# Half mixers in two streams: turning and angles in every second portion, products in the others

## The chip, the cores and the metric

The kernel runs on one core of one Trainium2 chip. The metric is the time of one execution on the device in microseconds (us); each kernel is run several times and the median is compared. Below, PE is TensorE, PEld its weight loads, DVE VectorE, ACT ScalarE, POOL GpSimd, SP SyncE, which issues DMAs. L368 is line 368 of the kernel before.

## What is computed

Eight batches of attention over 576 positions with 8 heads of width 64. In each row of scores only the 32 largest count. The result goes through a mixer with 512 channels, whose weights are one set for all batches. All of it is float32.

```python
scores = scale * q @ k.T                       # 576 x 576 for each head
attn = softmax(where(scores >= 32nd largest of the row, scores, -1e9))
x = attn @ v                                   # heads side by side: 576 x 512
theta = x @ w_theta
y = w_tok_r @ (x * cos(theta)) + w_tok_i @ (x * sin(theta))
u = x + y
out = u + relu(u @ w_ch)
```

## The kernel before

**Units.** Attention is cut into units of 128 queries of a pair of heads (two score rows of 576 in each partition); the last unit of a pair holds the 64 queries left over, of both heads. A batch has 20 units, the kernel 160. `GROUPS` gives the order within a batch: all five units of pair 0, then the first two of pairs 1 and 2, all five of pair 3, then the last three of pairs 1 and 2. So the queries of the first half (blocks 0 and 1, h = 0) are complete after unit 10 of a batch, those of the second (blocks 2, 3 and the rest, h = 1) after unit 19.

**Steps.** `pipeline` runs one iteration per unit, and each iteration emits steps of several units in the order `ORDER`: P (`penalize`: ACT makes a penalty, POOL subtracts it), T and Z (`threshold`: DVE finds the 32nd largest), U (`turn`: PE transposes the exponentials of the unit before the last, ACT copies them out of PSUM), F (`pick`), K (`keep`: ACT copies a finished product with the values to `xt`), S (`scores` and `fold` of the unit three ahead), V (`mix_values`: product with the values into `px`), M (weights, at the start only), X (`exponent`: ACT, with the sums). Loads of the pairs, their split into high and low parts and the copies into place follow on SP's queue. Eleven buffers of tag `e` hold scores, exponentials and the raw pairs.

**Half mixers.** When the fourth pair of a half is kept (step K), a generator `mixer(bt, h)` is appended to the list `running`. It has two phases:
- turning and angles: for each block the sums get a tiny addend on POOL and DVE takes the reciprocal (L477, L478), PE turns `xt` (`px_s`, L621), DVE scales it into `z` (L515), PE turns it back (`px_t`, L530), ACT copies to `xt` (L532), PE multiplies by `w_theta` (`pth`, `angles`, L558 and L562), ACT and DVE take the fraction of a turn (`fraction`, L574 with the tile `whole`, and L575). Then `trig` does two sines and an absolute value per block on ACT (L583 to L585) and two multiplications on POOL (L586, L591). For h = 1, POOL first adds `part`, the share of the first half (L635).
- products: token products in `py` (L687), 32 of them for h = 0 and 40 for h = 1, of 256 or 320 columns; DVE or ACT takes each finished group of 4 or 5 (`settle`, L662 and L660). For h = 1 follow 32 channel products in `po` (L718); DVE adds and clamps (`give`, L669) into the output tile `ot`, and SP sends it out (L671).

**The order of the work.** Step U calls `advance` twice. Each call draws steps from the first generator of `running` until `RATE / 2` = 4.25 is used up; a product counts its columns over 288, a step of the turning counts `TURN` = 4.25. There is one stream: a half mixer is emitted whole before the next one begins, its sines are followed at once by its products. Two kinds of instructions keep the order in which they were emitted: the transposes of step U and the matmuls of the half mixers on PE (`fixed`), and exponentials and sines on ACT (`tabled`). The rest is ordered by a planner that works through the program with its own estimate of the times, and that prefers the mixer's steps somewhat (`M_REST`).

**Buffers that the change and the argument touch.** `ps_m`, two PSUM buffers, serves `px`, `pth`, `py` and `po`. `whole` and `ot` are one tile in one buffer (tag `ot`). `z0` and `z1` hold one half each, in one buffer. `zt` holds first the sines, then `part`.

The last half mixer (last batch, h = 1) is written another way (`split`): in fast float32 passes over high and low parts, and it runs after all the units.

Of the kernel before, what the change touches and what calls it, by code (L numbers as in the profile page):

```python
# [9 lines left out]
F32 = mybir.dt.float32  # L10
# [8 lines left out]
P = 128  # L19
EBUFS = 11  # L20
NQP = 1
WSTART = 2
AHEAD = 3
S_LATE = 0
RATE = 8.5
TURN = 4.25
ORDER = "PTUFKSTVMXZ"
FOLDS = 4
# [6 lines left out]
M_REST = -100  # L35
# [11 lines left out]
def topk_attention_phase_mixer(  # L47
# [11 lines left out]
    nc = tc.nc  # L59
    B, NPAIR, _, S = qT.shape  # L60
    DM = w_ch.shape[0]
# [3 lines left out]
    NJ = S // P  # L65
    REM = S - NJ * P
# [13 lines left out]
    wk2 = ctx.enter_context(tc.tile_pool(name="wk2", bufs=2))  # L80
# [97 lines left out]
    def later(n):  # L178
        return tc.high_priority(offset=-n)
# [283 lines left out]
    def mixer(bt, h, split=False, beside=False):  # L463
        bq, xt, sums, sums_rem = bt["bq"], bt["xt"], bt["sums"][h], bt["sums_rem"]
        js, j0 = HALVES[h], HALVES[h][0]
        x0 = j0 * P
        full = [j for j in js if j < NJ]
        nf = len(full)
        rinv = wk2.tile([P, len(js), H], F32, tag=f"rinv{h}", name=f"rinv{h}")
# [5 lines left out]
        for rows, ks in regions:  # L475
            tiny = least[:rows].to_broadcast([rows, ks.stop - ks.start, H])
            nc.gpsimd.tensor_add(sums[:rows, ks], sums[:rows, ks], tiny)  # L477
            nc.vector.reciprocal(rinv[:rows, ks], sums[:rows, ks])  # L478

        z = one.tile([P, 2 * nf + len(js) - nf, DM], F32, tag=f"z{h}", name=f"z{h}")  # L480
        zt = []
        if split:
            end = wk2.tile([P, NJ, P], F32, tag="vt", name="end").rearrange("p a b -> p (a b)")
# [81 lines left out]
                            )  # L565

        def fraction(j):
            whole = wk2.tile([P, S], F32, tag="ot", name="whole", bufs=1)[:, :DM]
            if j == NJ:
                last[0] = whole  # L570
            _, zr, _ = spots(j)
            n = zr.shape[-1]
            m = zr.shape[0]
            nc.scalar.activation(whole[:m, :n], th[j][:m, :n], AF.Identity, bias=magic[:m])  # L574
            nc.vector.scalar_tensor_tensor(  # L575
                zr, whole[:m, :n], MAGIC, th[j][:m, :n], op0=ALU.subtract, op1=ALU.subtract
            )
# [36 lines left out]
        for k in range(len(js) + 3):  # L614
            if k < len(js):
                rows = P if js[k] < NJ else REM
                px = ps_t.tile([P, DM], F32, tag="t", name="px_s")
                with later(M_PE):
                    for p in range(NB):
                        fill(  # L620
                            nc.tensor.transpose(  # L621
                                px[:rows, p * P : p * P + P], xt[h][:, p, k * P : k * P + rows], ident
                            )
                        )
                normalize(js[k], px)
            if 0 <= k - 3 < len(js):
                fraction(js[k - 3])
            if 0 <= k - 2 < len(js):
                angles(js[k - 2])
                yield TURN  # L630
            if 0 <= k - 1 < len(js):
                turn_back(js[k - 1])
            yield TURN if k <= len(js) else 0
        if h:
            nc.gpsimd.tensor_add(xt[1], xt[1], bt["part"])  # L635
        trig()
        yield 0
        if not h:
            bt["part"] = spare().rearrange("p (m n) -> p m n", n=QN[1])

# [27 lines left out]
        def give(m, c, ot, y):  # L668
            nc.vector.scalar_tensor_tensor(ot[:, spans[c]], y, 0.0, xt[c][:, m], op0=ALU.max, op1=ALU.add)  # L669
            if c == 1:  # L670
                nc.sync.dma_start(outT[bq, m * P : m * P + P], ot)  # L671

        for m in range(NB):
            for c in range(2):
# [18 lines left out]
                    flush(1)  # L693
        flush()
        if not h:
            return
        for m in range(NB):
            if not split:
                ot = wk2.tile([P, S], F32, tag="ot", name="ot", bufs=1)
            else:  # L700
                if m % 2 == 0:
                    ots = wk2.tile([P, 2, S], F32, tag="kh", name="ots")
                ot = ots[:, m % 2]
            for c in range(2):
                cs, n = spans[c], QN[c]
                po = accumulator(m, c, "po")
                ms = slice(m * P, m * P + P)
                if split:
                    mm = []
                    for kb in range(NB):  # L710
                        mm += passes(
                            *(w[kb][:, ms] for w in w_parts["ch"]), x_hi[c][:, kb], x_lo[kb // 2][:, kb % 2, cs]
                        )
                else:
                    mm = [(wts["ch"][kb][:, ms], xt[c][:, kb]) for kb in range(NB)]
                for i, (l, r) in enumerate(mm):
                    with later(M_TOK if split else 0):
                        fill(nc.tensor.matmul(po[:, :n], l, r, start=(i == 0), stop=(i == len(mm) - 1)))  # L718
                    if not split:
                        yield n / HS  # L720
                        flush()
                late.append(lambda m=m, c=c, o=ot, y=po[:, :n]: give(m, c, o, y))
                if split:
                    flush()
        flush()

    def new_batch(bq):
        sums = [wk2.tile([P, len(js), H], F32, tag=f"sums{h}", name=f"sums{h}") for h, js in enumerate(HALVES)]
        sums_rem = wk2.tile([P, NPAIR], F32, tag="sums_rem", name="sums_rem")
        return dict(bq=bq, sums=sums, sums_rem=sums_rem, xt=[None, None], done=[0, 0])  # L730

    flag = const.tile([1, 1], I32, name="flag")

    def pipeline():
# [6 lines left out]
                plan += [(len(groups) - 1, j) for j in range(ja, jb)]  # L741
        total, per_batch = len(plan), len(plan) // B
        starts = [g[3] for g in groups] + [total]
        units, pairs, batches, running, budget = {}, {}, {}, [], [0.0]
        todo = {}

        def unit(i):
            if not 0 <= i < total:
                return None
            if i not in units:  # L750
                g, j = plan[i]
                b, p = groups[g][:2]
                if b not in batches:
                    batches[b] = new_batch(b)
                    if b % MARKED:
                        batches[b]["marks"] = batches[b - 1]["marks"]
                slot = (b % MARKED * NPAIR + p) * (2 * NJ + 1) + 2 * j
                units[i] = Unit(b, batches[b], p, j, pairs[g], slot, False)
            return units[i]
# [16 lines left out]
            ):  # L776
                todo.setdefault(max(at, 0), []).append((work, g))

        def advance(share):
            budget[0] = min(budget[0] + share, share) if running else 0.0  # L780
            while running and budget[0] > 0:
                with later(M_REST):
                    done = next(running[0], None)
                if done is None:
                    running.pop(0)
                else:
                    budget[0] -= done

# [4 lines left out]
            fold(unit(i))  # L793
        pick(unit(0))
        for i in range(total + 3):
            now, nxt, old, last = unit(i), unit(i + 1), unit(i - 1), unit(i - 2)
            parts = threshold(now) if now else iter(())

            def keep():
                u = unit(i - 3)  # L800
                if u:
                    h = keep_values(u)
                    if h is not None:
                        end = u.bq == B - 1 and h == 1
                        running.append(mixer(u.batch, h, end, not end))

            def ahead():
                if unit(i + AHEAD):
                    with later(S_LATE):
                        scores(unit(i + AHEAD))  # L810
                        fold(unit(i + AHEAD))

            steps = {
                "P": lambda: old and penalize(old),
                "F": lambda: nxt and pick(nxt),
                "T": lambda: next(parts, None),
                "Z": lambda: list(parts),
                "U": lambda: last and turn(last, unit(i - 3), lambda: advance(RATE / 2)),
                "K": keep,
                "S": ahead,  # L820
                "V": lambda: last and mix_values(last),
                "M": lambda: [next(wsteps, None) for _ in range(2 - i % 2)],
                "X": lambda: old and exponent(old),
            }
            for c in ORDER:
                steps[c]()
            done = unit(i - 2)
            if done and (i - 1) % per_batch == 0 and done.bq % MARKED == MARKED - 1:
                judge(done.batch["marks"], done.bq // MARKED)
            for work, g in todo.get(i, ()):  # L830
                work(g)
# [4 lines left out]
        nc.tensor.transpose(pf[:1, :P], worst[:, :1], ident)  # L836
        nc.vector.reduce_max(flag_f, pf[:1, :P], axis=AX.X)
        nc.vector.tensor_copy(flag, flag_f)
        for m in running:
            for _ in m:  # L840
                pass

# [68 lines left out]
```

## Time and profile before

| | us |
|---|---|
| median of 3 runs | 1411.42 (1411.14 to 1418.38) |
| the profiled execution | 1409.92 |
| its span, first to last instruction | 1408.1 |
| PE, DVE, ACT, POOL busy in the span | 1190.7, 1140.4, 1055.4, 726.8 |
| mean granted clock of TensorE | 0.929 of full speed |

A window is a stretch of the span in us from its start. A row of the trace gives first what was busy, then in brackets or behind a bar how long the engine was idle just before and what ended that idle time. PE's busy time counts a matmul from its issue to its modelled end, and matmuls overlap, so the sum of their durations is more than the busy time.

### The profile page before, as it was taken

The numbers are of one execution on the slowest core, as the hardware profiler recorded it, in microseconds if no ns is written. First come the engines' busy times: TensorE is split into PE (matmuls) and PEld (weight loads), VectorE is DVE, ScalarE is ACT, GpSimd is POOL, SyncE is SP. The second block draws the span as 40 slices with busy tenths as digits, with TensorE's granted clock in tenths as the row PEclk, the third lists the DMA queues.
The fourth block names the chain that finished last, engine by engine and source line by source line (L and its number), as shares of the span: only waits on it lengthen the run. The fifth ranks groups of instructions, "written<-read, shape, count | busy, mean of one in ns | idle before, by whom it ended". The sixth has DMA issues, their size and how long they took to land.

```text
span 1408.1 us, 23356 instructions
## 1 busy us (share of the span) xinstructions
PE 1190.7 (85%) x6253; PEld 866.3 (62%) x6253; DVE 1140.4 (81%) x5050; ACT 1055.4 (75%) x2152; POOL 726.8 (52%) x986
## 2 busy tenths in 40 slices
PE   4667788997979989798789979899898988799778
PEld 3445465775657666576566756577565756476458
DVE  7999889789897878879797788979888798977133
ACT  5999696966879486875969668885879769696551
POOL 4688564744556254652737436472546526463340
PEclk9777899999989999999898999899998999999899
DMA  6657233344434342253333434333423534321000
GB/s 176 172 143 205 73 99 85 78 115 104 113 73 100 90 114 73 73 144 92 91 83 78 114 97 111 86 94 87 122 73 73 145 91 114 82 68 43 9 1 36
DMA packets 101996, 134.47 MB, mean 95 GB/s; under 512 B 20320, under 2 KB 59488, under 8 KB 101856
## 3 DMA queue, kind: packets, MB, share of 16 engines
q1 hardware_dynamic: 101856, 132.90, 36.6%
q8 instruction: 52, 0.85, 0.3%
q14 instruction: 88, 0.72, 0.2%
HBM read 47.84 MB, written 9.44 MB: 41 GB/s over the span
## 4 chain that ended last, share of the span: by engine, by line
ACT 28%; PE 25%; DVE 22%; DMA 8%; POOL 6%; issue 6%; SPq 5%; ACTq 0%; POOLq 0%; DVEq 0%
ACT e L368 7%; PE py L687 6%; PE pth L558 5%; PE px L413 5%; ACT pen L355 5%; DVE lst L309 4%; DVE lst L331 4%; POOL e L357 4%; DVE best L325 4%; SPq L230 4%; ACT e L274 3%; PE ps_score L265 3%; PE pt L383 3%; PE po L718 2%; DVE lo L302 2%
## 5 line engine op out<-in xcount | busy, mean ns | idle before, releaser
L357 POOL TENSOR_TENSOR e<-e,pen 128x576 f32<-128x576 f32 x288 | 364.7, 1282 | 132.2 <-ACT pen L355 130.9
L687 PE MATMUL py<-w,z 128*128 128x256 f32 (+1 forms) x1072 | 316.4, 431 | 49.0 <-POOL z L591 46.0
L325 DVE MAX8 best<-lst 128x8 f32<-128x122 f32 (+3 forms) x1152 | 284.0, 287 | 23.5 <-POOL lim L336 22.5
L687 PEld LDWEIGHTS py<-w,z 128*128 128x128 f32 x1072 | 200.7, 201 | 96.1 <-POOL z L591 51.3
L265 PE MATMUL ps_score<-kh,q 128*128 128x288 f32 x512 | 187.4, 379 | 77.4 <-DVE lo L304 45.9
L368 ACT ACTIVATE e<-e,lim 128x576 f32<-128x576 f32 x288 | 223.0, 775 | 26.2 <-POOL e L357 24.8
L331 DVE MATCH_REPLACE8 lst<-best,lst 128x122 f32<-128x122 f32 (+2 forms) x864 | 230.9, 273 | 0.2
L355 ACT ACTIVATE pen<-e,lim 128x576 bf16<-128x576 f32 x288 | 209.5, 770 | 26.7 <-POOL lim L336 23.0
L309 DVE MAX8 lst<-lo 128x8 f32<-128x72 f32 (+1 forms) x864 | 208.5, 292 | 0.1
L383 PE MATMUL pt<-ident,e 128*128 128x128 f32 x1152 | 186.9, 287 | 18.3 <-ACT at L385 8.0
L274 ACT COPY e<-ps_score 128x576 f32<-128x576 f32 x256 | 158.6, 640 | 54.5 <-PE ps_score L265 37.5
L383 PEld LDWEIGHTS pt<-ident,e 128*128 128x128 f32 x1152 | 145.7, 147 | 73.2 <-issue 19.9
L385 ACT COPY at<-pt 128x512 f32<-128x512 f32 x256 | 148.6, 584 | 37.7 <-PE pt L383 35.0
L413 PE MATMUL px<-at,vt 128*64 128x320 f32 (+1 forms) x1024 | 167.5, 450 | 6.6 <-ACT at L388 4.2
L265 PEld LDWEIGHTS ps_score<-kh,q 128*128 128x128 f32 x512 | 104.3, 204 | 101.7 <-issue 42.7
L265 PE MATMUL ps_score<-kl,q 128*128 128x288 f32 x512 | 155.5, 317 | 10.8 <-DMA kl<-raw 10.8
L301 DVE TENSOR_TENSOR ps_score<-ps_score,e 128x288 f32<-128x288 f32 (+1 forms) x160 | 68.3, 427 | 78.7 <-ACT e L274 68.1
L218 POOL TENSOR_TENSOR raw<-raw,hi 128x832 fp32r<-128x832 f32 (+2 forms) x47 | 104.6, 2226 | 52.5 <-ACT hi L217 51.6
L413 PEld LDWEIGHTS px<-at,vt 128*64 128x64 f32 x1024 | 80.0, 149 | 74.6 <-issue 26.8
L718 PE MATMUL po<-xt,w 128*128 128x256 f32 (+1 forms) x448 | 120.7, 407 | 1.6 <-DVE xt L662 1.4
L558 PE MATMUL pth<-w,xt 128*128 128x512 f32 x240 | 111.9, 610 | 8.2 <-ACT xt L532 8.2
L312 POOL COPY marks<-lst 128x6 f32<-128x6 f32 (+1 forms) x160 | 31.1, 195 | 168.5 <-DVE lst L309 164.1
(136 smaller groups left out, 2017.2 us busy)
## 6 DMA issues: line engine op xcount, KB each, us to landing
kh<-hi SPq DMA_DIRECT2D x188, 144.0 KB, 2.5
kl<-raw SPq DMA_DIRECT2D x188, 144.0 KB, 2.6
raw<-in_kT_dram SPq DMA_DIRECT2D x47, 288.0 KB, 3.1
vt<-in_v_dram SPq DMA_DIRECT2D x48, 256.0 KB, 3.0
out_dram<-ot SPq DMA_DIRECT2D x28, 288.0 KB, 2.1
raw<-in_qT_dram SPq DMA_DIRECT2D x15, 288.0 KB, 3.0
q<-hi SPq DMA_DIRECT2D x30, 144.0 KB, 2.8
q<-raw SPq DMA_DIRECT2D x30, 144.0 KB, 2.8
```

The source lines that it names most:

```text
L265: nc.tensor.matmul(out[:, at : at + n], l, r, start=(i == 0), stop=(i == len(mm) - 1), skip_group_check=True)
L274: nc.scalar.copy(u.x[:, :, keys], u.ps[:, :, :HS])
L309: nc.vector.max(u.lst[:, w, QS + i * 8 : QS + i * 8 + 8], u.lo1[:, w, lo:hi])
L325: nc.vector.max(top[:, w, best], part[w])
L331: nc.vector.match_replace(out=rest, in_to_replace=top[:, w, best], in_values=part[w], imm_value=LOWEST)
L355: nc.scalar.activation(pen[:, w], u.x[:, w], AF.Relu, bias=u.lim[:, w, 0:1], scale=-STEEP)
L357: nc.gpsimd.tensor_sub(u.x[:, w], u.x[:, w], pen[:, w])
L368: nc.scalar.activation(u.x[:, w], u.x[:, w], AF.Exp, bias=u.lim[:, w, 1:2], scale=SCALE, accum_out=acc)
L383: fixed(nc.tensor.transpose(pt[:, c], e[:, w, at0 : at0 + P], ident))
L413: nc.tensor.matmul(px[sl, :n], pr["vt"][:, kb, sl], pr["at"][:, a, kb], start=(kb == 0), stop=False, skip_group_check=True)
L558: fill(nc.tensor.matmul(th[j][: l.shape[-1]], l, r, **pos))
L687: fill(nc.tensor.matmul(py[:, :n], l, r, start=(i == 0), stop=(i == len(mm) - 1)))
```

## The change

There are two lists in the place of `running`: `turning` and `products`. Calls of `advance` alternate. Every second call draws one step of 4.25 from the first turning generator, if there is one; the others draw products, with `RATE` = 9.0, so 4.5 a call. While a first half (h = 0) is at its products, they are emitted in the others alone; products of a second half also take the turning calls that nothing is left for. After `trig` a generator moves to `products`, ready one unit later (`LAG`). The second half's sines wait, in the order of emission, until the first half's products are done (`added`), since these make `part`. In the last batch (`hurry`) both kinds take any call. The reciprocals come one step after POOL's addition; `whole` has a tile of its own; the second half's output is made in the tile `z1`, in four places; and the output DMAs of all but the last half mixer are issued by POOL in the place of SP. The number of instructions that compute is the same.

```diff
-RATE = 8.5
+RATE = 9.0
+LAG = 1
...
             nc.gpsimd.tensor_add(sums[:rows, ks], sums[:rows, ks], tiny)
-            nc.vector.reciprocal(rinv[:rows, ks], sums[:rows, ks])
+        yield 0
+        nc.vector.reciprocal(rinv[:, :nf], sums[:, :nf])
+        if NJ in js:
+            nc.vector.reciprocal(rinv[:REM, nf:], sums[:REM, nf:])
...
-            whole = wk2.tile([P, S], F32, tag="ot", name="whole", bufs=1)[:, :DM]
+            whole = wk2.tile([P, DM], F32, tag="whole", name="whole", bufs=1)
...
+        while h and not bt["added"]:
+            yield None
         if h:
             nc.gpsimd.tensor_add(xt[1], xt[1], bt["part"])
         trig()
-        yield 0
+        yield "turned"
...
-                nc.sync.dma_start(outT[bq, m * P : m * P + P], ot)
+                (nc.sync if split else nc.gpsimd).dma_start(outT[bq, m * P : m * P + P], ot)
...
         if not h:
+            bt["added"] = True
             return
...
-                ot = wk2.tile([P, S], F32, tag="ot", name="ot", bufs=1)
+                ot = z.rearrange("p k d -> p (k d)")[:, m * S : m * S + S]
...
-        def advance(share):
-            budget[0] = min(budget[0] + share, share) if running else 0.0
-            while running and budget[0] > 0:
+        def turned(share):
+            while turning and share > 0:
                 with later(M_REST):
-                    done = next(running[0], None)
+                    done = next(turning[0][0], "turned")
                 if done is None:
-                    running.pop(0)
+                    return False
+                if done == "turned":
+                    m, h = turning.pop(0)
+                    products.append((m, clock[0] + LAG, h))
+                    return True
+                share -= done
+            return bool(turning)
+
+        def advance(share, hurry):
+            budget[1] = not budget[1]
+            ready = products and products[0][1] <= clock[0]
+            first_half = ready and products[0][2] == 0
+            if (budget[1] or hurry and not ready) and turned(TURN):
+                return
+            if budget[1] and first_half and not hurry:
+                return
+            budget[0] = min(budget[0] + share, share) if ready else 0.0
+            while products and products[0][1] <= clock[0] and budget[0] > 0:
+                with later(M_REST):
+                    done = next(products[0][0], None)
+                if done is None:
+                    products.pop(0)
                 else:
                     budget[0] -= done
...
                         end = u.bq == B - 1 and h == 1
-                        running.append(mixer(u.batch, h, end, not end))
+                        mixers = mixer(u.batch, h, end, not end)
+                        if not end:
+                            next(mixers)
+                        turning.append((mixers, h))
...
-                "U": lambda: last and turn(last, unit(i - 3), lambda: advance(RATE / 2)),
+                "U": lambda: last and turn(last, unit(i - 3), lambda: advance(RATE / 2, last.bq == B - 1)),
```

## Rows read from the trace of the kernel before

**Rows 1.** The page's first part: busy time, share of the span and instructions, of the two busiest engines.

```profile
PE 1190.7 (85%) x6253; PEld 866.3 (62%) x6253; DVE 1140.4 (81%) x5050; ACT 1055.4 (75%) x2152; POOL 726.8 (52%) x986
```

**Rows 2.** Windows over the whole span: first the stretches of three batches in the middle, then one batch from sines to sines of the second half, then the end. Columns: window, its length, busy time (instructions) of PE, PEld, DVE, ACT and POOL, granted clock, share of the DMA engines, GB/s.

```profile
160.00:325.00 165.00, 147.08 (x786) 107.06 (x786) 139.02 (x618) 129.88 (x266) 86.33 (x120) 0.96 0.38 96
...
654.00:819.00 165.00, 145.96 (x778) 106.02 (x776) 140.01 (x636) 125.83 (x255) 82.34 (x117) 0.93 0.37 94
...
1144.00:1306.00 162.00, 141.57 (x754) 100.96 (x754) 131.33 (x592) 126.59 (x260) 80.80 (x115) 0.95 0.31 80
...
737.00:900.00 163.00, 145.44 (x772) 105.27 (x772) 134.21 (x604) 125.44 (x258) 83.54 (x118) 0.95 0.38 97
...
1306.00:1350.00 44.00, 34.92 (x175) 24.15 (x172) 6.10 (x12) 25.09 (x53) 16.52 (x17) 0.92 0.02 7
```

**Rows 3.** Windows over that batch by what the half mixers do, same columns: the second half's turning (712), its sines (737), token products (743) and channel products (782); the first half's turning (809), sines (822) and products (834); a stretch with no mixer (864); the next turning (874).

```profile
712.00:737.00 25.00, 22.75 (x137) 15.55 (x135) 24.96 (x107) 14.05 (x30) 6.92 (x8) 1.00 0.18 47
737.00:743.00 6.00, 2.83 (x8) 2.01 (x8) 6.00 (x30) 5.76 (x11) 2.48 (x5) 0.54 0.86 213
743.00:782.00 39.00, 38.03 (x200) 27.66 (x200) 26.35 (x125) 35.77 (x77) 26.07 (x40) 0.94 0.31 77
782.00:809.00 27.00, 25.97 (x148) 20.97 (x147) 22.74 (x98) 16.58 (x31) 12.52 (x16) 1.00 0.41 110
809.00:822.00 13.00, 11.07 (x66) 7.18 (x64) 13.00 (x54) 5.90 (x12) 2.49 (x5) 1.00 0.20 61
822.00:834.00 12.00, 9.14 (x45) 5.99 (x43) 8.81 (x46) 9.31 (x17) 3.45 (x6) 1.00 0.71 176
834.00:864.00 30.00, 26.70 (x129) 20.34 (x129) 24.73 (x119) 27.43 (x59) 19.00 (x30) 0.89 0.31 79
864.00:874.00 10.00, 7.47 (x48) 4.93 (x47) 7.78 (x31) 9.76 (x22) 7.67 (x8) 1.00 0.70 170
874.00:900.00 26.00, 24.24 (x141) 16.20 (x139) 24.81 (x107) 14.94 (x33) 9.87 (x13) 1.00 0.25 59
```

**Rows 4.** The same windows for the exponentials alone (L368; every one counts two instructions, itself and the reading of its sum).

```profile
743.00:782.00 39.00, 17.14 (x39) 0.94 0.31 77
782.00:809.00 27.00, 1.73 (x4) 1.00 0.41 110
809.00:822.00 13.00, 0.00 (x0) 1.00 0.20 61
822.00:834.00 12.00, 0.00 (x0) 1.00 0.71 176
834.00:864.00 30.00, 12.92 (x29) 0.89 0.31 79
```

**Rows 5.** Timeline of PE at the sines of the second half: start, duration, what, and in brackets the idle time before and its releaser.

```profile
738.25 0.58 PE L265 MATMUL ps_score<-kh,q 128*128 128x288 f32 x1 [2.94 <-DVE lo L304]
...
743.47 2.07 PE L687 MATMUL py<-w,z 128*128 128x256 f32 x4 [0.37 <-POOL z L591]
```

**Rows 6.** The waits, longest first: who waited for whom, us in total, times, longest.

```profile
ACT whole L574 <- PE pth L558: 81.5, 30, 4.3
...
DVE xt L662 <- PE py L687: 50.2, 37, 5.0
...
PE py L687 <- POOL z L591: 46.0, 16, 8.6
...
DVE z L575 <- ACT whole L574: 27.2, 11, 8.3
...
DVE rinv L478 <- POOL sums L477: 21.7, 10, 10.2
...
DVE ot L669 <- DMA out_dram<-ot: 12.0, 6, 4.1
```

**Rows 7.** Groups of instructions by line: shapes, count, busy time, mean ns of one, idle time before them and its releasers. The token products of all but the last half mixer.

```profile
L687 PE MATMUL py<-w,z 128*128 128x256 f32 (+1 forms) x1072 | 316.4, 431 | 49.0 <-POOL z L591 46.0 <-ACT xt L425 1.8 <-ACT zt L660 1.0
```

**Rows 8.** The chain of work that ended last, at two places: start, time that it took, what. Ten matmul instructions of the token products in a row, and an output DMA.

```profile
755.39 2.27 PE py L687 x10
...
790.82 3.45 DMA out_dram<-ot
```

**Rows 9.** The queue's own waits of SP, before the output DMAs (L671).

```profile
SPq L671 <- DVE lst L331: 45.8, 10, 8.1
SPq L671 <- DVE ot L669: 39.4, 9, 7.8
...
SPq L671 <- DVE best L325: 16.6, 5, 9.2
```

**Rows 10.** Line L671 by itself: duration of an issue (ns, least, median, most), first and last.

```profile
L671 SPq DMA_DIRECT2D out_dram<-ot x28: 332/344/1403, 295.7 to 1295.9; - x28
```

**Rows 11.** Three lines by themselves, with durations in ns (least, median, most): POOL's subtraction, DVE's settling and ACT's copy of `px`.

```profile
L357 POOL TENSOR_TENSOR e<-e,pen x288: 1271/1282/1297, 33.9 to 1326.8; 128x576 f32<-128x576 f32 x144
...
L662 DVE TENSOR_TENSOR xt<-py,xt x96: 399/424/492, 180.9 to 1388.9; 128x256 f32<-128x256 f32 x64, 128x320 f32<-128x320 f32 x32
...
L425 ACT COPY xt<-px x64: 346/393/429, 56.0 to 1351.1; 128x256 f32<-128x256 f32 x32, 128x320 f32<-128x320 f32 x32
```

More of the change, by code (lines that the diff above doesn't have):

```diff
@@ L729, in new_batch @@
         sums_rem = wk2.tile([P, NPAIR], F32, tag="sums_rem", name="sums_rem")
-        return dict(bq=bq, sums=sums, sums_rem=sums_rem, xt=[None, None], done=[0, 0])
+        return dict(bq=bq, sums=sums, sums_rem=sums_rem, xt=[None, None], done=[0, 0], added=False)
     flag = const.tile([1, 1], I32, name="flag")
@@ L743, in pipeline @@
         starts = [g[3] for g in groups] + [total]
-        units, pairs, batches, running, budget = {}, {}, {}, [], [0.0]
+        units, pairs, batches, turning, products, budget, clock = {}, {}, {}, [], [], [0.0, False], [0]
         todo = {}
@@ L795, in pipeline @@
         for i in range(total + 3):
+            clock[0] = i
             now, nxt, old, last = unit(i), unit(i + 1), unit(i - 1), unit(i - 2)
@@ L838, in pipeline @@
         nc.vector.tensor_copy(flag, flag_f)
-        for m in running:
+        for m in [m[0] for m in products + turning]:
             for _ in m:
```

## The prediction

> **What bounds the kernel now.** I read the busy times first. PE has work in 85% of the span and DVE in 81% [rows 1], so no engine is the bound by itself. The windows by batch show that the kernel is periodic: a batch takes 162 to 165 us, of which PE is busy 145 and DVE 134 to 140 [rows 2]. The windows within one batch show why neither is full: the limit changes hands [rows 3]. While the second half is turned, DVE is busy without a break (24.96 of 25 us, 24.81 of 26), and PE has about 2 us left over. In the token products PE is busy 38.03 of 39 us and DVE 26.35; in the channel products PE 25.97 of 27. Between these lie stretches in which neither is full: the sines (PE 2.83 of 6 us, 9.14 of 12) and the 10 us without a mixer (7.47). PE is idle 18 us of the 163 in sum, DVE 29 [rows 2].
>
> The rest of the reading is on what opens the gaps. The waits name them [rows 6]: PE waits 46.0 us before token products for POOL's multiplications behind the sines (16 times, 2.9 us each); DVE waits 21.7 us for the sums, 27.2 for `whole`, 12.0 for an output DMA that must leave `ot` free; ACT waits 81.5 us for `pth`. The timeline at one of the sines shows the first: score matmuls one by one behind idle gaps of up to 2.94 us, then products that begin when the multiplication ends [rows 5]. After such gaps the granted clock is low: 0.54 in the 6 us of the sines, 0.94 and 0.89 in the two product stretches behind sines, 1.00 elsewhere [rows 3].
>
> The exponentials show a further bound. 39 instructions of them lie in the 39 us after the second half's sines, then 4, 0 and 0 in the next 52 us, then 29 after the first half's sines [rows 4]. Exponentials and sines keep the order of emission, so ACT runs ahead in the products and then stands until the next sines are through.
>
> **The change, part by part.** Walking the portions by hand through one batch (unit numbers from the batch's start): before, the second half is turned in units 23 to 26, with sines and products in 26 and on to 34; the first half's turning takes 34 to 36, its products 37 to 41; nothing lies in 42. After: the second half is turned in 43 to 49, one step a unit, beside the first half's products (42 to 48); sines in 50; its products alone in 51 to 53, beside the next first half's turning in 54 to 59, alone in 60 to 62. The period stays 20 units. So it fits, nothing piles up, and the sum of work per batch is unchanged. What can be won is idle time. Working per batch, of 163 us:
>
> *The wait for the sines.* 46.0 us over 16 halves is 2.9 each, 5.8 a batch [rows 6]. A unit (163 / 20 = 8.2 us) now lies between, and the first half's sines have second-half products beside them. What is late next: the transposes of the following unit are ahead of those products on PE and need exponentials that stand behind the sines on ACT. Ends 0 and -5.8; I take -3.5, nearer to the full gain, since POOL's multiplications drop out of the path for certain.
>
> *The clock behind these gaps.* 6 us at 0.54, 39 at 0.94 and 30 at 0.89 lose 2.8 + 2.3 + 3.3 = 8.4 us of full clock [rows 3]. Ends 0 and -8.4; I take -2, since those gaps have other causes too (DVE's fold in [rows 5]). The Trainium skill ("TensorE: Matmul & The Clock Gate", Part 1) has the clock fall to half after an idle window of about 3.4 us and return after as much work; the 0.54 behind a gap of 2.94 us agrees. By it alone a gap that is closed gives all of it back, an estimate of -8.4.
>
> *DVE's waits.* The reciprocal comes a step later, so DVE need not stand for the sums: 21.7 / 8 = 2.7 a batch. Four places for the output and a `whole` of its own remove the wait for the DMA: 12.0 / 7 = 1.7. `fraction` now comes two units after its `angles` in place of one: 27.2 / 8 = 3.4 [rows 6]. Together 7.8. Ends 0 and -7.8; I take -3, since in products DVE has 12 us to spare of 39 [rows 3], and there it is hidden. ACT's 81.5 us before `whole` goes the same way; I cost it at nothing, as ACT is busy 125 of 163 us [rows 2]; were it to fill, its waits would be in the terms above.
>
> *Heavier portions.* Ten matmul instructions took 2.27 us [rows 8], and a product is two of them (1072 [rows 7] for 8 x 32 + 7 x 40 = 536): 0.45 us. 4.5 for 4.25 adds 2 x 0.25 x 0.45 = 0.2 us in each unit with two product portions, some 6 a batch. The work is not more, only denser: 0 to +1.4; I take +0.5.
>
> *Two PSUM buffers for both streams.* `pth` is held from a block's angles to its fraction, now two units, and the next angles follow at once. So in about 5 units of the second half's turning and 3 of the first's, one of the two `ps_m` buffers is taken, and `py` and `px` hand the other to and fro. No row shows this. A handover is at least the settling, 0.42 us [rows 11], and at most that, the mean wait for `py`, 50.2 / 37 = 1.36 [rows 6], and a copy of `px`, 0.39 [rows 11]: 2.2 us. Eight handovers: 0 (scores run meanwhile) to +17.6. I take +1, from the nearest row: with `px` in one buffer and `py` in the other, which products have now, PE waited 1.8 us in all for that copy [rows 7].
>
> *Output DMAs on POOL.* Each issue took 0.34 us on SP [rows 10]; 4 x 0.34 = 1.4 us more on POOL, which is busy 84 of 163 [rows 2]. Behind it on POOL stand the subtractions before the exponentials and the limits. On SP, loads no longer stand behind it (the chain runs through an output DMA of 3.45 us [rows 8]). On POOL the issue will wait for `give`, as it did on SP: 45.8 + 39.4 + 16.6 = 101.8 us in 24 waits, 4.2 each [rows 9]. Ends -3.45 and +16.8 a batch; I take 0, as POOL has time.
>
> The sum is -3.5 - 2 - 3 + 0.5 + 1 + 0 = -7.0 a batch, 156 us for 163. PE would be busy 145 of 156, 93%, which it surpasses now in the products (97%), so it isn't beyond reach. Seven such periods lie between 160 and 1306 us: -49.
>
> *The end.* Before, all but the last half mixer is emitted by unit 161 of the walk. After, the products of batch 6's second half end there, seven units later than now, and 22 of the last first half's 32 products are left for behind the loop. At unit 154, 39 product counts more are open than before: 39 x 0.45 = 17.6 us. PE is idle 9.1 of the 44 us there [rows 2]. Ends 0 and +17.6; I take +9, half hidden in that idle time.
>
> 1409.9 (the profiled execution, 1.5 below the median) - 49 + 9 = **1370 us**.
>
> **The rivals.**
> - *The wait moves, no more.* PE no longer waits for POOL, but transposes wait for exponentials behind the sines, as [rows 4] bear out, and the planner lays the rest as before. Then -1.5 a batch: 1409.9 - 10 + 9 = 1409. Against it: the output DMA, `whole` and the sums are waits of other kinds.
> - *PSUM.* Half of the eight handovers show: +8.8 in place of +1, so +0.8 a batch: 1409.9 + 6 + 9 = 1425. All of them: +9.6 x 7 + 9, 1486. It decides from 0.84 us shown per handover (7 x (8 x 0.84 - 8) + 9 = 0). For it: DVE is in order and full in turning. Against it: scores aren't bound to the order and fill PE.
> - *POOL's queue.* All 28 outputs wait 4.2 us, 118 us, with the subtractions behind them. From a third on (39 us) the gain is gone; at half, 1370 + 59 = 1429. Against it: POOL waits for DVE in any case at that place. Its subtractions last 1271 to 1297 ns beside any DVE work [rows 11]. The Trainium skill ("SBUF — State Buffer", the box on DVE and DMA under "SBUF: two separate sides", and the one on bandwidth) says that a DMA issued by GpSimd needs descriptors that GpSimd can't write while VectorE holds their shared port: 0.62 us alone, 3.1 beside a copy. By it an estimate of 28 x 2.5 = 70 us on POOL, the same direction; no row here shows such a DMA.
> - *Two full engines.* DVE goes from 134 to 140 us of work a batch to about 97% of the time: 144 a batch, -19 x 7 + 9: 1286; more likely halfway, 1290 to 1335.
>
> **How the numbers follow.** Forecast (1335 to 1403) 0.56, two full engines 0.05, the wait moves 0.13, PSUM 0.16, POOL 0.10. Measurement tells about 0.5%, 7 us, from no change. Faster is 0.56 + 0.05 = 0.61, same 0.13, slower 0.26. The range reaches from 1335 to 1440: left out are the 0.05 below and the worse part of PSUM and POOL above, about 0.13.
>
> **What would show it.** Right: a period near 156 us; PE's wait for POOL's multiplications below 15 us; DVE's waits for the sums and the output near zero; windows in which PE and DVE are busy alike instead of in turn; a longer stretch of products after DVE's last threshold. Wrong: PE idle before `py` or `px` with DVE's settling, ACT's copy or ACT's `whole` as releaser (PSUM); POOL standing at the output DMAs with `penalize` behind; idle time before transposes on exponentials of the same size as the wait removed.

## The result and the profile after

The changed kernel takes 1337.01 us (median of 4 runs, 1335.57 to 1341.53), the kernel before 1413.43 (4 runs); the ratio is 0.946, 95% interval 0.9424 to 0.9497. The forecast was 1370, with a range from 1335 to 1440: the direction held and the time lies just inside the lower end. The medians differ by 76 us. The account below goes by the profiled spans, which differ by 68, where the sum had 40; the profiled execution of the changed kernel (1341.53) is the slowest of its four.

The page's first part of the changed kernel, beside [rows 1]: the work is the same, and every engine's share is up. PE's busy time itself is shorter by 26.6 us, and the mean granted clock is 0.947 for 0.929.

```profile
PE 1164.1 (87%) x6253; PEld 858.3 (64%) x6253; DVE 1136.0 (85%) x5050; ACT 1052.6 (79%) x2152; POOL 744.8 (56%) x1014
```

Windows by batch of the changed kernel, columns as in [rows 2]; the last but one goes from sines to sines of the second half as the window 737 to 900 does there, and the last is the end.

```profile
469.00:623.00 154.00, 140.74 (x777) 103.87 (x778) 137.62 (x626) 125.91 (x259) 86.59 (x122) 0.98 0.41 103
623.00:776.00 153.00, 139.54 (x766) 101.81 (x765) 138.03 (x622) 124.14 (x256) 85.53 (x122) 0.98 0.40 102
...
718.00:872.00 154.00, 140.69 (x778) 103.39 (x778) 137.17 (x624) 125.88 (x259) 86.23 (x122) 0.98 0.40 103
...
1239.00:1340.00 101.00, 85.33 (x478) 68.83 (x476) 37.47 (x63) 38.76 (x76) 29.87 (x25) 0.96 0.07 25
```

These batches take 153 and 154 us in place of 162 to 165. Of the 9 us between 163 and 154, PE's idle time gives 17.6 - 13.3 = 4.3, and PE's busy time 145.4 - 140.7 = 4.7: nearly the same matmuls at a clock of 0.98 for 0.95. That is one batch; seven of them, below, share it out otherwise.

Windows within that batch, beside [rows 3]: the second half's sines, and what waits for them, are at 719 to 733; products alone to 757; then turning of the next first half beside products, with its sines near 776; products alone to 812; the next second half's turning beside the first half's products to 854.

```profile
719.00:725.00 6.00, 4.24 (x26) 2.55 (x24) 5.28 (x28) 5.63 (x12) 2.08 (x3) 1.00 0.67 158
725.00:733.00 8.00, 4.07 (x14) 3.32 (x15) 6.17 (x28) 7.97 (x18) 5.39 (x11) 0.62 0.43 118
733.00:757.00 24.00, 23.86 (x134) 18.78 (x133) 17.87 (x86) 20.51 (x44) 14.46 (x19) 0.98 0.31 75
757.00:776.00 19.00, 18.27 (x97) 12.50 (x96) 19.00 (x86) 13.81 (x29) 10.78 (x15) 1.00 0.41 104
776.00:782.00 6.00, 4.47 (x30) 3.97 (x29) 4.82 (x21) 5.32 (x9) 2.41 (x3) 1.00 0.42 108
782.00:790.00 8.00, 8.00 (x37) 5.38 (x36) 8.00 (x42) 5.14 (x11) 4.02 (x7) 1.00 0.44 100
790.00:812.00 22.00, 20.59 (x114) 14.92 (x114) 20.38 (x90) 21.55 (x46) 16.15 (x26) 1.00 0.53 151
...
830.00:854.00 24.00, 22.97 (x130) 17.21 (x130) 23.95 (x111) 18.34 (x41) 12.45 (x17) 1.00 0.35 84
```

In the mixed stretches (757 to 776, 830 to 854) PE and DVE are both at 95% or more, which no stretch of [rows 3] shows for both at once. The first half's sines leave no dip of the clock any more (1.00 at 776 and in the windows behind it); the second half's still do (0.62 at 725). In the unit between there is no other half's work, and that is the likely reason.

The waits of the changed kernel, beside [rows 6]. PE's wait for POOL's multiplications (46.0 us) and DVE's for the output DMA (12.0) are gone from the list. DVE's wait for the sums is not: it stands at two lines now, 8.0 + 7.5 = 15.5 us for 21.7. One has grown: PE's transposes wait 26.6 us for exponentials, which stand behind the sines on ACT; before, that was 6.8 us.

```profile
ACT whole L578 <- PE pth L562: 53.6, 29, 3.8
...
DVE xt L668 <- PE py L693: 46.0, 25, 4.1
...
PE pt L384 <- ACT e L369: 26.6, 13, 3.0
...
POOL out_dram L677 <- DVE z L675: 18.1, 9, 8.6
...
DVE z L579 <- ACT whole L578: 13.3, 4, 9.6
...
DVE rinv L481 <- POOL sums L478: 8.0, 7, 2.6
DVE rinv L483 <- POOL sums L478: 7.5, 7, 1.7
```

One more of PE's waits fell nearly as much as the one for POOL: the scores' wait for DVE's fold, first before, then in the changed kernel.

```profile
PE ps_score L265 <- DVE lo L304: 48.7, 22, 5.3
```

```profile
PE ps_score L266 <- DVE lo L305: 10.2, 8, 3.8
```

Where in the span the 68 us come from can be read from a mark that stands at the same unit in both kernels: ACT's copies of `px` (64 of them, eight to a batch). These are the 7th (unit 16 of the first batch) and the 63rd (the same unit of the last). The timeline of ACT, first the kernel before, then the changed one: start, duration, what.

```profile
196.87 0.43 ACT L425 COPY xt<-px 128x320 f32<-128x320 f32 x1
...
1337.73 0.42 ACT L425 COPY xt<-px 128x320 f32<-128x320 f32 x1
```

```profile
179.08 0.44 ACT L426 COPY xt<-px 128x320 f32<-128x320 f32 x1
...
1259.14 0.44 ACT L426 COPY xt<-px 128x320 f32<-128x320 f32 x1
```

Windows over the three stretches that these marks make (columns as in [rows 2]), before and changed:

```profile
0.00:196.87 196.87, 131.09 (x576) 92.72 (x577) 175.70 (x801) 160.85 (x323) 130.89 (x174) 0.83 0.55 147
196.87:1337.73 1140.86, 1002.95 (x5335) 724.30 (x5334) 940.94 (x4204) 872.37 (x1786) 579.05 (x802) 0.95 0.36 91
1337.73:1408.10 70.37, 56.66 (x346) 49.31 (x344) 23.78 (x46) 22.17 (x44) 16.90 (x11) 0.94 0.05 19
```

```profile
0.00:179.08 179.08, 117.60 (x521) 81.51 (x521) 162.62 (x741) 150.40 (x302) 122.98 (x158) 0.81 0.58 154
179.08:1259.14 1080.06, 979.21 (x5341) 719.69 (x5342) 939.99 (x4256) 879.54 (x1806) 602.55 (x844) 0.97 0.38 97
1259.14:1339.90 80.76, 67.25 (x392) 57.06 (x391) 33.38 (x54) 22.66 (x46) 19.27 (x13) 0.95 0.06 24
```

| stretch, us | before | changed | difference | of it PE busy | of it PE idle |
|---|---|---|---|---|---|
| start to the 7th copy | 196.87 | 179.08 | -17.8 | -13.5 | -4.3 |
| seven batches, to the 63rd copy | 1140.86 | 1080.06 | -60.8 (-8.7 each) | -23.7 (-3.4 each) | -37.1 (-5.3 each) |
| from there to the end of the span | 70.37 | 80.76 | +10.4 | +10.6 | -0.2 |

### The profile page after: what moved, and what is told of

The parts are those of the page before. It is cut to its first block, busy times and chain, and to the rows that moved or that the text cites. A ratio compares the mean times of both kernels' runs of the same rounds, so it can differ in the third digit from the quotient of the medians.

```text
span 1339.9 us, 23360 instructions
## 1 busy us (share of the span) xinstructions
PE 1164.1 (87%) x6253; PEld 858.3 (64%) x6253; DVE 1136.0 (85%) x5050; ACT 1052.6 (79%) x2152; POOL 744.8 (56%) x1014
## 4 chain that ended last, share of the span: by engine, by line
PE 39%; ACT 23%; DVE 18%; DMA 7%; SPq 5%; issue 4%; POOL 3%; ACTq 0%; POOLq 0%; DVEq 0%
PE py L693 12%; PE px L414 6%; ACT e L369 5%; PE ps_score L266 5%; PE pt L384 5%; SPq L231 5%; PE pth L562 4%; DMA q<-raw 3%; DVE lst L332 3%; DVE lst L310 3%; ACT e L275 3%; ACT pen L356 3%; DVE best L326 3%; PE po L725 3%; ACT at L386 2%
## 5 line engine op out<-in xcount | busy, mean ns | idle before, releaser
L693 PE MATMUL py<-w,z 128*128 128x256 f32 (+1 forms) x1072 | 300.9, 424 | 1.7 <-ACT zt L666 1.2
L384 PE MATMUL pt<-ident,e 128*128 128x128 f32 x1152 | 189.0, 289 | 61.2 <-ACT e L369 26.6
L693 PEld LDWEIGHTS py<-w,z 128*128 128x128 f32 x1072 | 203.5, 200 | 47.3 <-ACT zt L666 1.4
L369 ACT ACTIVATE e<-e,lim 128x576 f32<-128x576 f32 x288 | 224.6, 781 | 11.3 <-POOL e L358 10.6
L332 DVE MATCH_REPLACE8 lst<-best,lst 128x158 f32<-128x158 f32 (+2 forms) x864 | 231.2, 274 | 0.0
L384 PEld LDWEIGHTS pt<-ident,e 128*128 128x128 f32 x1152 | 142.3, 147 | 112.5 <-ACT e L369 30.2
L414 PE MATMUL px<-at,vt 128*64 128x320 f32 (+1 forms) x1024 | 157.3, 432 | 12.5 <-ACT at L386 10.4
L414 PEld LDWEIGHTS px<-at,vt 128*64 128x64 f32 x1024 | 73.7, 143 | 72.6 <-ACT at L386 14.9
L562 PE MATMUL pth<-w,xt 128*128 128x512 f32 x240 | 108.7, 595 | 2.9 <-ACT xt L426 2.9
L266 PEld LDWEIGHTS ps_score<-kl,q 128*128 128x128 f32 x512 | 104.9, 205 | 7.8 <-DMA kl<-raw 2.6
```

What stands on the lines that cost most here:

```text
L266: nc.tensor.matmul(out[:, at : at + n], l, r, start=(i == 0), stop=(i == len(mm) - 1), skip_group_check=True)
L332: nc.vector.match_replace(out=rest, in_to_replace=top[:, w, best], in_values=part[w], imm_value=LOWEST)
L369: nc.scalar.activation(u.x[:, w], u.x[:, w], AF.Exp, bias=u.lim[:, w, 1:2], scale=SCALE, accum_out=acc)
L384: fixed(nc.tensor.transpose(pt[:, c], e[:, w, at0 : at0 + P], ident))
L414: nc.tensor.matmul(px[sl, :n], pr["vt"][:, kb, sl], pr["at"][:, a, kb], start=(kb == 0), stop=False, skip_group_check=True)
L693: fill(nc.tensor.matmul(py[:, :n], l, r, start=(i == 0), stop=(i == len(mm) - 1)))
```

## The experiments

Two theories stood first. **S**: the two streams make the gain, since work lies between sines and products and PE's and DVE's loads lie beside each other. **W**: the waits on buffers and queues (output, sums, fraction) make it.

**The side edits without the streams** (e1): the kernel before with this.

```diff
-            nc.vector.reciprocal(rinv[:rows, ks], sums[:rows, ks])
+        yield 0
+        nc.vector.reciprocal(rinv[:, :nf], sums[:, :nf])
+        if NJ in js:
+            nc.vector.reciprocal(rinv[:REM, nf:], sums[:REM, nf:])
-            whole = wk2.tile([P, S], F32, tag="ot", name="whole", bufs=1)[:, :DM]
+            whole = wk2.tile([P, DM], F32, tag="whole", name="whole", bufs=1)
-                ot = wk2.tile([P, S], F32, tag="ot", name="ot", bufs=1)
+                ot = z.rearrange("p k d -> p (k d)")[:, m * S : m * S + S]
-                nc.sync.dma_start(outT[bq, m * P : m * P + P], ot)
+                (nc.sync if split else nc.gpsimd).dma_start(outT[bq, m * P : m * P + P], ot)
-                        running.append(mixer(u.batch, h, end, not end))
+                        mixers = mixer(u.batch, h, end, not end)
+                        if not end:
+                            next(mixers)
+                        running.append(mixers)
```

> The kernel before with one stream as it was, and only the side edits: reciprocals a step later, a tile of its own for the fraction (whole), the output in z1 and its DMAs on POOL. Theory S (the two streams make the gain, since they lay PE's and DVE's loads side by side and put work between sines and products): -5 to -20 us, 1393 to 1408, and PE still waits over 35 us for POOL's multiplications. Rival W (the waits on the output buffer, the sums and the fraction make it): -35 us or more, 1378 or less.

1410.35 us, ratio 0.9988 (0.9963 to 1.0012): no change that shows, less than even S had said. Its waits, columns as in [rows 6]:

```profile
PE py L690 <- POOL z L594: 42.7, 16, 7.9
DVE rinv L480 <- POOL sums L477: 18.4, 10, 10.2
...
POOL out_dram L674 <- DVE lst L331: 7.4, 10, 2.6
...
DVE rinv L482 <- POOL sums L477: 3.9, 1, 3.9
```

DVE no longer waits for the output DMA, and that was worth nothing. Its wait for the sums stayed, 18.4 + 3.9 = 22.3 us for 21.7: in one stream a step later is not late enough. So this run says nothing of what that wait is worth.

**The streams without the outputs on POOL and the later reciprocals** (e2): the changed kernel with

```diff
-                (nc.sync if split else nc.gpsimd).dma_start(outT[bq, m * P : m * P + P], ot)
+                nc.sync.dma_start(outT[bq, m * P : m * P + P], ot)
```

and the reciprocals back in their loop, ahead of the new `yield 0`:

```diff
+            nc.vector.reciprocal(rinv[:rows, ks], sums[:rows, ks])
         yield 0
-
-        nc.vector.reciprocal(rinv[:, :nf], sums[:, :nf])
-        if NJ in js:
-            nc.vector.reciprocal(rinv[:REM, nf:], sums[:REM, nf:])
```

> The changed kernel with the output DMAs back on SP and the reciprocals at once behind POOL's addition; the streams, the unit between, the tile for the fraction and the output in z1 stay. Theory S: 1340 to 1352, nearly all of the gain. Rival W: 1365 or more, since the waits of DVE for the sums (21.7 us before) and of the loads behind the outputs on SP come back.

1338.98 us, ratio 0.949 (0.946 to 0.9521): the whole gain, a little more than S had said. DVE's wait for the sums is what it is in the changed kernel, 15.0 us for 15.5:

```profile
DVE rinv L479 <- POOL sums L478: 15.0, 14, 2.6
```

With e1 this decides for S: neither the outputs on POOL nor the later reciprocals make the gain. The later reciprocals did not even shorten their wait; that it fell from 21.7 to 15 us goes with the streams.

**Two buffers alone** (e3): the kernel before with only the two tile lines of e1.

> The kernel before with only the tile of its own for the fraction and the output in z1 (DMAs on SP, reciprocals at once). Theory S: 1400 to 1411; DVE's 12 us before the output are gone and little else. Rival W: 1385 or less.

1412.06 us, 0.9993 (0.9973 to 1.0014): no change. No run has the streams with `whole` and the output in one buffer, as before.

**No unit between** (e4): the changed kernel with

```diff
-LAG = 1
+LAG = 0
```

> The changed kernel with LAG 0: a half's products may follow its sines in the same unit. By the walk only the second half's products move, by one unit; the first half's stand behind the second half's products anyway. If the unit between is what keeps PE from waiting: PE waits about 3 to 6 us per second half for POOL's multiplications again, 20 to 40 us in all, and the time is 1350 to 1375. Rival (the alternation alone does it, the wait goes to the exponentials behind the sines in either case): 1334 to 1345.

1369.4 us, 0.969 (0.9664 to 0.9716): the first theory's number. The waits of this run:

```profile
PE py L693 <- DMA z<-whole: 19.5, 5, 4.6
...
PE py L693 <- POOL z L595: 13.2, 14, 5.4
...
PE pt L384 <- ACT e L369: 7.2, 5, 2.9
```

PE waits 19.5 + 13.2 = 32.7 us before products, and the kernel is 32 us slower than the changed one. That the two numbers agree is chance: the transposes' wait is back at 7.2 us, and PE's idle time in all is only 10 us longer (1369.9 - 1183.8 = 186.1 for 175.8). The other 20 of the 30 us between the profiled spans are PE's busy time, 1183.8 us for 1164.1, at a mean clock of 0.937 for 0.947. More than half of the wait before products is for the DMA that puts the results of the last block's multiplications in place, a step that the prediction did not count.

**One stream with a hold** (e5), and the same density without it (e6): the kernel before with `RATE = 9.5`, and in e5

```diff
-        yield 0
+        yield 0 if split else "turned"
...
+            if hold[0] > clock[0]:
+                return
...
+                elif done == "turned":
+                    hold[0], budget[0] = clock[0] + 1, 0.0
```

> The kernel before, one stream, with a hold: after its sines a half mixer gives nothing until the next unit; RATE 9.5 so that two halves still fit in 20 units. If PE's wait for the sines is the whole gain: 1335 to 1360. If the gain needs two streams, because a hold in one stream is a hole in PE's work: 1385 to 1410, with PE's wait for POOL's multiplications near zero all the same.

> The kernel before with RATE 9.5 and nothing else, to set beside the run with the hold. Both theories: 1400 to 1420, as the portions are denser but the work is the same.

1434.97 us, 1.0154 (1.0107 to 1.0202), and 1432.83, 1.0111 (1.0057 to 1.0165). The hold did what it should: PE's wait for POOL's multiplications, 70.4 us in e6, is gone in e5. The time stayed: the hold gained nothing, and the density alone had made one stream 1.1% slower. Neither theory expected that; both runs lie above every range that was set for them. In e5 the wait stands elsewhere:

```profile
ACT whole L574 <- PE pth L558: 93.4, 32, 4.7
DVE z L575 <- ACT whole L574: 58.3, 13, 6.7
...
PE pt L383 <- ACT e L368: 32.3, 19, 5.3
```

So in one stream taking the wait away is no gain; what the second stream adds is the other half's work in that time.

**Nine buffers of tag e** (e7 in the kernel before, e8 in the changed one):

```diff
-EBUFS = 11
+EBUFS = 9
```

> The kernel before with 9 in place of 11 buffers of tag e. Theory S (before, the limit changes hands between PE and DVE and the buffers carry one over the other's stretch): 1440 or more, at least 25 us more loss than the changed kernel has with 9. Rival (buffers matter alike in both): the same loss in both within 10 us.

> The changed kernel with 9 in place of 11 buffers of tag e. Theory S (its loads lie side by side, so less must be carried over): 1337 to 1355. Rival: as much loss as the kernel before has with 9.

Before: 1414.12 us, 1.0001 (0.9976 to 1.0027). Changed: 1345.85, 0.9528 (0.9482 to 0.9573), some 9 us more than with eleven (the two intervals of the ratio overlap). This part of theory S fell: the kernel before does not live on these buffers. The changed one may use them a little.

**Two lists and the unit between, but no alternation** (e9): the changed kernel with

```diff
-            if (budget[1] or hurry and not ready) and turned(TURN):
-                return
-            if budget[1] and first_half and not hurry:
-                return
+            if turned(TURN):
+                return
```

> The changed kernel with two lists and the unit between, but no alternation: turning takes every call as long as there is any, products have the rest (turning again in 3.5 and 2.5 units, one unit without products behind the second half's sines). If filling the gap behind the sines is all: 1334 to 1350. If the alternation (turning beside products) carries a part of its own: 1360 to 1390, with stretches of full DVE and of full PE in turn as before.

1378.31 us, 0.9737 (0.9695 to 0.9779): alternation has a part of its own. Windows of this run, from sines to sines of the second half, then its parts: the sines (725), products (733), the next first half's turning (780) and sines (801), products (813), the second half's turning (855).

```profile
725.00:882.00 157.00, 144.44 (x782) 105.43 (x779) 135.77 (x607) 126.16 (x258) 86.87 (x122) 0.96 0.40 102
...
725.00:733.00 8.00, 4.73 (x24) 2.41 (x20) 8.00 (x36) 6.71 (x14) 4.87 (x7) 0.92 0.79 201
733.00:780.00 47.00, 44.68 (x243) 35.55 (x243) 35.58 (x165) 42.16 (x86) 31.61 (x46) 0.94 0.44 110
780.00:801.00 21.00, 20.27 (x121) 14.52 (x122) 20.79 (x90) 12.07 (x25) 5.72 (x11) 1.00 0.15 50
...
813.00:855.00 42.00, 39.68 (x204) 30.43 (x204) 35.49 (x171) 39.81 (x87) 28.87 (x41) 0.92 0.44 117
```

PE's idle time is about as short as in the changed kernel (157 - 144.4 = 12.6 for 13.3), but PE is busy 3.7 us longer for nearly the same matmuls. The clock of 0.94 and 0.92 is a mean. It is low only in the first 7 or 8 us of each stretch, behind the sines, and full in the rest:

```profile
733.00:740.00 7.00, 4.68 (x17) 3.82 (x17) 2.28 (x15) 6.97 (x16) 3.83 (x9) 0.60 0.22 56
740.00:780.00 40.00, 40.00 (x228) 31.73 (x227) 33.29 (x151) 35.20 (x71) 27.79 (x37) 1.00 0.48 120
813.00:821.00 8.00, 6.91 (x22) 5.67 (x23) 6.13 (x37) 7.25 (x16) 4.68 (x8) 0.57 0.18 55
```

So e9 has two such stretches in a batch, one behind each half's sines, and the changed kernel has one.

By the marks (7th copy at 196.94, 63rd at 1307.53, span 1378.9) this run has nothing at the start, -4.3 us a batch and +1.0 at the end. In e4 (176.78, 1289.84, 1369.9) it is -20.1, -4.0 a batch and +9.7. So the start and the end go with the alternation, which puts products off. In total each batch gets some 4 us by the alternation and some 5 by the unit between, but not each in its own way. The seven batches of e4, then of e9:

```profile
176.78:1289.84 1113.06, 1001.05 (x5349) 730.99 (x5350) 944.48 (x4257) 883.20 (x1807) 602.02 (x845) 0.95 0.37 95
```

```profile
196.94:1307.53 1110.59, 1005.59 (x5335) 734.38 (x5334) 942.76 (x4214) 877.25 (x1794) 597.59 (x835) 0.94 0.37 94
```

| us a batch | PE busy | PE idle |
|---|---|---|
| before | 143.3 | 19.7 |
| alternation, no unit between (e4) | 143.0 | 16.0 |
| unit between, no alternation (e9) | 143.7 | 15.0 |
| changed | 139.9 | 14.4 |

Either one shortens PE's idle time and leaves its busy time as it was. The 3.4 us of busy time, at the higher clock, come only with both.

**The fraction a step sooner** (e10): the changed kernel with `fraction` moved from behind the next block's transposes to the step behind its own angles.

```diff
-            if 0 <= k - 3 < len(js):
-                fraction(js[k - 3])
             if 0 <= k - 2 < len(js):
                 angles(js[k - 2])
                 yield TURN
+            if 0 <= k - 2 < len(js):
+                fraction(js[k - 2])
```

> The changed kernel with each block's fraction emitted one step (one unit) behind its angles and no longer two, so that pth gives its PSUM buffer back a unit sooner. If the two buffers for both streams cost something (the PSUM rival, which the prediction priced at +1 us a batch): 1325 to 1333. If they cost nothing: 1335 to 1345, or slower where ACT and DVE again wait for pth.

1338.35 us, 0.9466 (0.9424 to 0.9508): the same as the changed kernel's 1337.0. Holding `pth` for two units costs nothing that shows. Nor does the second unit give anything: DVE's wait for `whole` is 13.3 us in both.

**Density** (e11, and e12 with 10.0) in the changed kernel:

```diff
-RATE = 9.0
+RATE = 8.5
```

> The changed kernel with RATE 8.5: lighter portions that end a unit later in the batch; two generators are left over at the end in place of one. If density costs (+0.5 us a batch in the prediction): 1330 to 1337 but for the end, which gets 3 to 8 us longer. If not: 1338 to 1350.

> The changed kernel with RATE 10: products done up to a unit and a half sooner, with more units without any, and less left over at the end. If density costs: 1342 to 1360. If the end counts more: 1328 to 1337.

1337.97 us, 0.9457 (0.9417 to 0.9497), and 1329.76, 0.9408 (0.9365 to 0.9451). By the marks a batch takes 152.6 and 153.1 us for 154.3, so neither way costs; the end takes 88.3 us with 8.5 (1336.0 - 1247.73) and 76.3 with 10 (1326.3 - 1249.96), for 80.8 with 9. The version with 10 is the fastest that ran. Its four runs (1327.9 to 1334.0) lie below the four of the changed kernel (1335.6 to 1341.5), though the two intervals of the ratio to the kernel before overlap.

## Why the prediction was right in direction and short in size

**The bound**, as read: neither engine full, and time lost where sines, products and turning meet. This held. That the limit changes hands was seen rightly, but e7 shows that it isn't the number of `e` buffers that couples the two.

**The wait for the sines** (-3.5 a batch): right, also in what is late next. 46.0 us are gone; the transposes' wait rose by 26.6 - 6.8 = 19.8. Over 16 halves, two to a batch, that is -5.8 + 2.5 = -3.3. But these are two of PE's waits among several. The scores' wait for DVE's fold fell from 48.7 to 10.2 us, -4.8 a batch, and no term had it; PE's other waits grew by some 23 us, the scores' for ACT's copies from 19.5 to 31.9 among them. In sum PE's idle time fell by 5.3 a batch. So it is in part luck that -3.3 lies so near the -3.5 of the sum. Why the fold's wait fell was not singled out; in e6 it is 12.5 us with one stream and no gain, beside the 70.4 for POOL.

**The clock** (-2, with ends 0 and -8.4): right in direction, mis-sized. PE's busy time for nearly the same matmuls fell by 3.4 us a batch over the seven, by 4.7 in the one of [rows 2]. The Trainium skill's rule ("TensorE: Matmul & The Clock Gate", Part 1), a fall after an idle window of about 3.4 us, gave the direction. The trace agrees with it in the low clock behind idle time, not in the length: no gap shown here is that long, the longest at these sines being 2.94 and 2.58 us. Its -8.4 was too much, since the second half's sines still leave a gap, with 0.62 behind it.

**DVE's waits** (-3): mis-sized, and one step of it failed. The reciprocal a step later was to end the wait for the sums; 15.5 of the 21.7 us are still there, as many as with the reciprocal at once (15.0 in e2). e1 removed the output's wait without gain, and e10 found nothing in the second unit before `fraction`. The longest of the output's waits, 4.1 us, lies in the channel products, where PE was busy 25.97 of 27 us [rows 3]; the term should have been near its end 0. What the sums' wait is worth no run shows.

**Density** (+0.5), **PSUM** (+1) and **POOL** (0): nothing in e11 and e12, e10, and e2. The issue on POOL takes 0.58 us for 0.34 on SP, and POOL waits 28 us in all at these outputs (18.1, 6.9 and 3.1 by the line's own view), but no one waits for them. The line by itself, ns as in [rows 10]:

```profile
L677 POOL DMA_DIRECT2D out_dram<-z x28: 539/580/726, 329.2 to 1265.8; - x28
```

The starving of such DMAs that the Trainium skill describes ("SBUF — State Buffer", the box on DVE and DMA under "SBUF: two separate sides") doesn't show here: they land in 2.7 us in the median, 4.6 at most, for 2.1 and 3.8 on SP. That box speaks of VectorE operations in a 2-port mode; no run here tells whether any stood beside these DMAs.

So a batch came to -5.3 of idle and -3.4 of busy time, -8.7 in place of -7.0, seven of them to -61 in place of -49.

**The end** (+9): +10.4, near in number, but not by the reasoning. The sum had 39 product counts left over at unit 154, half of them hidden in PE's idle time. From the mark on, a little later, 46 PE instructions more stand there than before, as many as 23 products have, and none is hidden: PE is busy 10.6 us longer and idle as long as before. **The step that failed** is the other side of this term. The end gets longer because products are put off, and the same work is then missing at the start. I counted seven periods from 160 us on and nothing before, so the start stood at 0 without a reason; it is 17.8 us shorter. In the kernel before, 48 matmuls of the token products lie ahead of the 7th copy, in the changed one none (in e9, which has nothing at the start, 42):

```profile
0.00:196.87 196.87, 14.57 (x48) 9.26 (x48) 1.24 (x3) 1.22 (x3) 0.83 0.55 147
```

Put off and given back, the deferral is -7.4 us net, where the sum had +9. With -61 for the batches that makes the 68 us.

The rivals: "the wait moves, no more" is what e5 shows for one stream; in two, less than half of the 46 us came back before the transposes. PSUM and POOL's queue cost nothing that shows. Two full engines was the better guide to the mixed stretches (95% and more of both), but not to the whole.

What stays open is which gaps let the clock fall. e9 has two low stretches in a batch and the changed kernel one, so what alternation adds is that the first half's sines, which lie among the second half's products, leave none. But gaps differ in length and in what stands around them, and no run here varies that alone.

## What to carry to other kernels

A unit of distance between a producer and its consumer is worth only what other work fills it: it gave 0 in one stream (e5 beside e6) and 32 us in two (e4). When work is put off, count both ends: what is missing at the start is as real as what is left over at the end. Price a removed wait by the stretch in which it lies: 12 us of DVE's waits taken away (e1) changed nothing, where PE was nearly full. And look in the trace whether the wait went at all: the later reciprocals left theirs as it was.

## What the runs showed of the hardware that was not expected

The granted clock made up two fifths of what a batch won: 3.4 of 8.7 us, PE's busy time for nearly the same matmuls, between 0.95 and 0.97 over the seven batches. Gaps shorter than 3 us go with a low clock: one of 2.94 us stands in the 6 us at 0.54 [rows 3, 5], and one of 2.58 us, with one of 1.42 just ahead of it, in the 8 us at 0.62 of the changed kernel. A gap of 1.52 us stands in a window at 1.00 (776 to 782). The timeline of PE in the changed kernel shows them (start, duration, what, idle time before and releaser):

```profile
726.36 0.40 PE L266 MATMUL ps_score<-kh,q 128*128 128x288 f32 x1 [1.42 <-ACT e L275]
729.79 1.12 PE L384 MATMUL pt<-ident,e 128*128 128x128 f32 x4 [2.58 <-ACT e L369]
...
779.30 0.66 PE L384 MATMUL pt<-ident,e 128*128 128x128 f32 x4 [1.52 <-ACT xt L536]
```
